# An attention and two-mixer kernel: first chunk's normalisation traced with heads 23 to 28, third batch's Fourier stage not hurried, last sums on VectorE

## The chip, the cores and the metric

One core of a Trainium2 chip. TensorE (PE) multiplies, VectorE (DVE), ScalarE (ACT) and GpSimd (POOL) work on tiles of 128 partitions, SyncE (SP) and others issue DMAs. The metric is the time of one execution on the device, in microseconds (us). The kernel before took 980.12 us (median of three runs, 977.31 to 981.54). About 0.5% (4.9 us) is what a measurement of this kernel can tell from no change.

## The reference

```python
x = attention(q, k, v, f)          # 4 batches, 8 heads, 576 positions, 64 wide; scores get a decay from cumsum(log f), causal softmax
# first mixer
X = np.fft.fft(np.fft.fft(x, axis=1), axis=2)
u = x + np.real(X)
un = (u - mean(u)) / np.sqrt(var(u) + 1e-06)         # over the 512 features
x = u + np.maximum(un @ w_ch1, 0.0) @ w_ch2          # 512 -> 2048 -> 512
# second mixer
theta = x @ w_theta
y = w_tok_r @ (x * cos(theta)) + w_tok_i @ (x * sin(theta))
u = x + y
out = u + np.maximum(u @ w_ch, 0.0)
```

## The kernel before

Features lie on partitions and positions along the free axis. The tile `u` (128 x 4 x 2304 floats) holds the result of the Fourier stage of all four batches, 576 columns each, from then on to the end.

The source is traced into one instruction list per engine. A planner orders each list: an instruction whose inputs and buffers are there may be placed ahead of others that were traced before it, those traced earlier (or marked `high_priority`) go first where both could start. On the chip each engine works through its own list in order and stops at an instruction that waits.

Phase 1 (`phase1`, lines 456 to 538) runs over n = -1 to 32. Turn n traces the scores of head n+1 (`score_units`: two matmul lines L232 and L233, the minimum on VectorE L241, Exp on ScalarE L246), the transposes of head n (`turn_units`, L271 and L274) and, every second turn, the product with v of a pair of heads (`av_units`, L303). After the pair, `evac_pair` scales it (L329, L335); for every odd pair it moves two rows by DMA through SP and forms the sum E and the difference O of the two pairs on GpSimd (L348, L350). After four pairs the Fourier stage of that batch (`fft_units`) starts as a generator. Each pass of the inner loop calls `pull()`, which takes one step of `rows` (evac_pair), one of `fft`, and on every third call one of `norm`. The Fourier stage folds E and O (L377, L381), splits them (L379 to L386), multiplies along the features (L406, L417) and along the positions (L429), and adds into `u` (L437 to L453), of which L447 is on GpSimd.

At n = 29 (line 510) the loop pulls until the Fourier stage of the third batch has been traced to its end. Only then its tiles E, O, yh, yl and zh can be taken for the normalisation of chunk 0. There are six chunks of 384 columns; chunk 0 lies in the first batch. `norm_units` (L689 to L716): three sums on GpSimd (L694 to L696), the mean by a matmul (L700), four subtractions on VectorE (L702), two squares on ScalarE (L705), three more sums on GpSimd (L706, L708), and the variance by three small matmuls (L713). `norm_end` follows: Sqrt on ScalarE (L720), reciprocal (L723), the spread of the three columns by matmuls (L725), and for each of four feature blocks a product (L732), a cast (L733) and a remainder (L734).

At n = 31 the pool of the heads' inputs closes and the weight loads open in its place: `decode` fetches half a weight block (L544, two `raw` buffers), takes it apart on ScalarE (L558), VectorE (L560, L561, L563, L565) and again ScalarE and VectorE (L570, L572). Phase 2 (`phase2`) traces the rest of the last batch's Fourier stage and then the matrix products of the first mixer, chunk by chunk, four weight blocks at a time: `ffn1` (L745, then the h tile by ACT L750 and DVE L751) and `ffn2` (L759, sums into u at L767). Phase 3 is the second mixer; the change does not touch it.

Of the kernel before, what the change touches and what calls it, by code (L numbers as in the profile page):

```python
# [8 lines left out]
F32 = mybir.dt.float32  # L9
# [3 lines left out]
AF = mybir.ActivationFunctionType  # L13
ALU = mybir.AluOpType
# [3 lines left out]
B, H, S, D = 4, 8, 576, 64  # L18
NP = 4
NF = 16  # L20
CH = 384
# [34 lines left out]
class Net:  # L56
    def __init__(self, ctx, tc, ins, out):
        self.ctx, self.tc, self.nc = ctx, tc, tc.nc
        self.i, self.out = ins, out
        nc = self.nc  # L60
        self.base = ctx.enter_context(tc.tile_pool(name="base", bufs=1))
        self.psa = ctx.enter_context(tc.tile_pool(name="psa", bufs=3, space=PSUM))
        self.psb = ctx.enter_context(tc.tile_pool(name="psb", bufs=3, space=PSUM))
        self.pt = ExitStack()
        self.pst = self.pt.enter_context(tc.tile_pool(name="pst", bufs=1, space=PSUM))
        self.nout = 0
        self.u = self.base.tile([128, 4, B * S], F32, name="u")
        self.ident = self.base.tile([128, 128], F32, name="ident")
        self.mean = self.base.tile([128, 128], F32, name="mean")
        nc.gpsimd.memset(self.mean, 1.0 / 512.0)  # L70
        self.eps = self.base.tile([128, 1], F32, name="eps")
        nc.gpsimd.memset(self.eps, 1e-6)
        self.un = {}
        self.stash = {}
        self.sdram = ctx.enter_context(tc.tile_pool(name="sdram", bufs=1, space=DRAM))
# [245 lines left out]
        yield  # L321
        done(m, T, R)

    def evac_pair(self, p, R, T):
        nc = self.nc
        k = p // 2
        if p % 2 == 0:
            self.X = R
            nc.vector.tensor_tensor(R, T[:, 256:832], R, ALU.mult)  # L329
            if k == 0:  # L330
                self.EO = [self.c1.tile([128, 2, S], F32, tag=x, name=x, bufs=2) for x in ("E", "O")]
            return
        X, (E, O) = self.X, self.EO
        Y = R
        nc.vector.tensor_tensor(Y, T[:, 256:832], R, ALU.mult)  # L335
        if k == 0:
            self.x384 = self.fdram.tile([1, S], F32, tag="x384", name="x384", bufs=2)
            nc.sync.dma_start(self.x384, Y[64:65])
            nc.sync.dma_start(Y[64:65], Y[0:1])
            nc.gpsimd.memset(Y[0:1], 0.0)  # L340
        else:
            self.x256 = self.c1.tile([1, S], F32, tag="x256", name="x256", bufs=1)
            nc.sync.dma_start(self.x256, Y[64:65])
            nc.sync.dma_start(Y[64:65], Y[0:1])
            nc.sync.dma_start(Y[0:1], self.x384)
        for _ in range(4):
            yield
        nc.gpsimd.tensor_tensor(E[:, k], X, Y, ALU.add)  # L348
        yield
        nc.gpsimd.tensor_tensor(O[:, k], X, Y, ALU.subtract)  # L350
        yield

    def fft_units(self, b, E, O, rows):
        nc = self.nc
# [36 lines left out]
        yh = w.tile([128, 3, 258], F32R, tag="yh", name="yh", bufs=1)  # L391
        yl = w.tile([128, 3, 258], F32R, tag="yl", name="yl", bufs=1)
# [4 lines left out]
        for s, (s0, me, mo) in enumerate(st):  # L397
            ps = self.bank_b()
# [33 lines left out]
        for t in range(2):  # L432
            ea = w.tile([128, S], F32, tag="ee", name="ea", bufs=1)
            oa = w.tile([128, S], F32, tag="oo", name="oa", bufs=1)
            ps = self.bank_b()
            fsum(ps, 128, yh, yl, cs, 128 * t, 128 * t + 128)
            nc.vector.scalar_tensor_tensor(ea[:, 0:289], E[:, t, 0:289], 0.5, ps[:, 0:289], ALU.mult, ALU.add)  # L437
            yield
            nc.vector.scalar_tensor_tensor(ea[:, 289:576], E[:, t, 289:576], 0.5, ps[:, 287:0:-1], ALU.mult, ALU.add)
            yield  # L440
            ps = self.bank_b()
            fsum(ps, 128, zh, zl, ss, 128 * t, 128 * t + 128)
            nc.vector.scalar_tensor_tensor(oa[:, 0:289], O[:, t, 0:289], -0.5, ps[:, 0:289], ALU.mult, ALU.add)
            yield
            nc.vector.scalar_tensor_tensor(oa[:, 289:576], O[:, t, 289:576], -0.5, ps[:, 287:0:-1], ALU.mult, ALU.subtract)
            (nc.vector if b == B - 1 or 1 >> t & 1 else nc.gpsimd).tensor_tensor(u[:, t, :], ea, oa, ALU.subtract)
            nc.gpsimd.tensor_tensor(u[:, 2 + t, :], ea, oa, ALU.add)  # L447
            for _ in range(1 if b == B - 1 or t else 7):
                yield
        ps = self.bank_b()  # L450
# [5 lines left out]
    def phase1(self):  # L456
        pair, heads = self.p1_open()
        NH = B * H
        pairs, heads, raws = {0: pair}, dict(enumerate(heads)), {}
        fft = None  # L460
        self.tick = 0
        rows, norm, av = iter(()), iter(()), iter(())

        def pull():
            nonlocal fft
            next(rows, 0)
            self.tick += 1
            if self.tick % 3 == 0:
                next(norm, 0)
            if (self.tick % 5 or n > 24) and fft is not None and next(fft, 0) == 0:  # L470
                fft = None

        def done(m, T, R):
            nonlocal rows, fft
            for _ in rows:
                pass
            rows = self.evac_pair(m % NP, R, T)
            next(rows, 0)
            if m % NP == NP - 1:
                fft = self.fft_units(m // NP, *self.EO, rows)  # L480

        for n in range(-1, NH + 1):
            a = self.score_units(heads[n + 1], (n + 1) % 2) if n + 1 < NH else iter(())
            prep = self.rest if n < 0 else iter(())
            if n + 2 < NH:
                p, g = divmod(n + 2, 2)
                if n == 0:
                    pairs[1] = self.load_pair(1)
                if n >= 0:
                    heads[n + 2] = dict(pair=pairs[p], g=n + 2)  # L490
                    prep = self.prep_units(n + 2, pairs[p], raws.pop(n + 2), heads[n + 2])
                if n > 0 and g == 1 and p + 1 < B * NP:
                    pairs[p + 1] = self.load_pair(p + 1)
            if n + 3 < NH:
                raws[n + 3] = self.load_head(n + 3)
            m, odd = divmod(n - 2, 2)
            if m >= 0 and not odd:
                T = self.bank_t()
                av = self.av_units(m, [heads[2 * m], heads[2 * m + 1]], T, pairs[m]["rz"], done)
            t = self.turn_units(heads[n]) if 0 <= n < NH else iter(())  # L500
            if n == NH - 1:
                self.p1a.close()
                self.p2_open()
                self.load(0)
                self.load(1)
            k = n - 2
            if 0 <= k < 4:
                for j in range(2):
                    self.load_dft(2 * k + j, f(heads[n]["hi"][0:1, 0, 0:2]))
            if n == NH - 3:  # L510
                while fft is not None:
                    pull()
                t1 = self.c1.tile([128, 2, CH], F32, tag="E", name="uc1", bufs=2)
                t2 = self.c1.tile([128, 2, CH], F32, tag="O", name="uc2", bufs=2)
                t3 = self.c1.tile([128, 2, CH], F32, tag="yh", name="s12", bufs=1)
                t4 = self.c1.tile([128, 2, CH], F32, tag="yl", name="sq", bufs=1)
                t5 = self.c1.tile([128, 4], F32, tag="zh", name="rs", bufs=1)
                norm = self.norm_units(0, ((t1, t2), t3[:, 0], t3[:, 1], t4, t5))
            live = True
            while live:  # L520
                live = False
                for g_ in (t, av, a):
                    if next(g_, 0) is None and (g_ is not av or n >= NH - 1):
                        live = True
                next(prep, 0)
                pull()
                if n >= NH - 1:
                    self.fill(2)
            for _ in prep:
                pass  # L530
        for _ in norm:
            pass
        self.p1b.close()
        for _ in rows:
            pass
        self.pt.close()
        self.pso = self.ctx.enter_context(self.tc.tile_pool(name="pso", bufs=2, space=PSUM))
        return fft
# [150 lines left out]
    def norm_units(self, c, temps):  # L689
# [22 lines left out]
        for k in range(3):  # L712
            nc.tensor.matmul(  # L713
                ps[:, 508 + k : 509 + k], s1[:, 128 * k : 128 * k + 128], self.mean[:, 0:1], start=True, stop=True
            )
        yield from self.norm_end(c, uc, rs, ps)  # L716

    def norm_end(self, c, uc, rs, ps):
        nc = self.nc
# [467 lines left out]
```

## Time and profile before

| what | value |
|---|---|
| median of three runs | 980.12 us (977.31 to 981.54) |
| the profiled execution | 974.18 us, its span 972.4 us |
| PE busy | 905.1 us (93% of the span) |
| DVE busy | 643.3 us (66%) |
| ACT busy | 426.1 us (44%) |
| POOL busy | 314.7 us (32%) |
| granted TensorE clock, mean of the span | 0.978 of full speed |

Shares of the whole span hide the stages. Phase 1 ends near 282 us, the first mixer has its first matmul at 284.05 us, and from about 369 us on PE is busy without a break to the end. Rows of the timeline give start and length in us, engine, line, operation, output and input; a bracket at the end is how long the engine stood idle before it, and what released it.

### The profile page before, as it was taken

Reading aid. Unit: us, or ns where it says so; the run is one execution under the profiler, and the core shown is the slowest. Engines: PE = TensorE matmul, PEld = TensorE weight load, DVE = VectorE, ACT = ScalarE, POOL = GpSimd, SP = SyncE. Lnnn points to the kernel's source line nnn. Section 1 sums busy time; section 2 is a strip of 40 time slices with the busy share of each in tenths; the row PEclk is TensorE's granted clock in tenths of the full one; section 3 lists DMA queues with packets and bytes.
Section 4 is the critical chain, followed back from the end, with each engine's and each line's share of the span. In section 5 each row is a group of like instructions: output and inputs, shape, how many; then the busy total and the mean of one; then the engine's idle time right before and its main releaser. Section 6 shows DMA issues by size and latency. Waiting matters only on the chain.

```text
span 972.4 us, 15900 instructions
## 1 busy us (share of the span) xinstructions
PE 905.1 (93%) x5960; PEld 850.8 (87%) x5960; DVE 643.3 (66%) x1503; ACT 426.1 (44%) x1038; POOL 314.7 (32%) x376
## 2 busy tenths in 40 slices
PE   3888898997978898999999999999999999999998
PEld 3667677776757798999999999999999999999998
DVE  7766777878789786535664466535677765746554
ACT  5777677767463342312322122212345534525331
POOL 4755457367433344200000000000014644525330
PEclk9998899999988999999999999999999999999999
DMA  4643223232132121002224022333420000010001
GB/s 145 200 131 123 70 86 102 89 101 67 36 108 67 44 87 44 1 1 77 76 65 145 30 87 87 112 108 106 138 62 1 1 25 26 2 37 14 25 26 49
DMA packets 24336, 68.04 MB, mean 70 GB/s; under 512 B 3534, under 2 KB 6990, under 8 KB 24260
## 3 DMA queue, kind: packets, MB, share of 16 engines
q1 hardware_dynamic: 20420, 62.52, 19.6%
q0 software_dynamic: 3120, 3.33, 1.4%
q10 hardware_dynamic: 720, 1.18, 0.4%
q8 instruction: 47, 0.77, 0.3%
q14 instruction: 29, 0.24, 0.1%
HBM read 57.92 MB, written 9.07 MB: 69 GB/s over the span
## 4 chain that ended last, share of the span: by engine, by line
PE 67%; DVE 18%; ACT 7%; issue 3%; POOL 2%; DMA 2%; ACTq 0%; DVEq 0%; POOLq 0%; SPq 0%
PE pa L745 19%; PE pb L759 11%; PE po L759 8%; PE pb L966 5%; PE pa L977 4%; PE pa L930 4%; PE pt L303 3%; ACT P L246 3%; PE po L966 3%; DVE P L241 2%; PE pb L271 2%; PE pa L232 2%; PE pa L233 2%; PE pb L429 1%; DVE kl L211 1%
## 5 line engine op out<-in xcount | busy, mean ns | idle before, releaser
L745 PE MATMUL pa<-un,wf 128*128 128x384 f32 x1152 | 222.8, 341 | 6.3 <-ACT wf L570 4.2
L745 PEld LDWEIGHTS pa<-un,wf 128*128 128x128 f32 x1152 | 204.4, 191 | 8.5 <-ACT wf L570 5.1
L751 DVE SCALAR_TENSOR_TENSOR h<-pa,h 128x384 fp32r<-128x384 f32 x96 | 53.1, 556 | 146.0 <-ACT h L750 146.0
L759 PE MATMUL pb<-h,wf 128*128 128x384 f32 x660 | 134.3, 336 | 0.3 <-DVE u L767 0.3
L759 PEld LDWEIGHTS pb<-h,wf 128*128 128x128 f32 x660 | 116.3, 188 | 0.9 <-DVE u L767 0.6
L750 ACT ACTIVATE h<-pa 128x384 fp32r<-128x384 f32 x96 | 46.8, 489 | 152.8 <-PE pa L745 152.7
L246 ACT ACTIVATE P<-P,mn 128x512 f32<-128x512 f32 (+4 forms) x160 | 95.7, 600 | 39.8 <-DVE mn L241 39.3
L759 PE MATMUL po<-h,wf 128*128 128x384 f32 x492 | 103.4, 339 | 4.1 <-DVE h L751 3.0
L232 PE MATMUL pa<-hi 128*128 128x448 f32 (+2 forms) x192 | 71.2, 390 | 30.8 <-DVE mn L241 16.1
L241 DVE CUSTOM_DVE_ANT_0 P<-pa,mask 128x512 f32<-128x512 f32 (+4 forms) x160 | 77.7, 510 | 30.6 <-PE pa L233 26.1
L966 PE MATMUL pb<-wtk,z 128*128 128x288 f32 x513 | 97.0, 294 | 0.0
L922 POOL COPY xd<-u 128x64 f32<-128x64 f32 x32 | 7.1, 265 | 272.2 <-DVE u L767 264.0
L759 PEld LDWEIGHTS po<-h,wf 128*128 128x128 f32 x492 | 87.5, 189 | 5.8 <-DVE h L751 3.4
L271 PE MATMUL pb<-ident,P 128*128 128x128 f32 x480 | 82.6, 288 | 7.4 <-ACT PT L274 4.3
L956 POOL TENSOR_TENSOR z<-kra,z 128x256 fp32r<-128x256 f32 x72 | 53.8, 767 | 86.8 <-ACT z L955 86.8
L966 PEld LDWEIGHTS pb<-wtk,z 128*128 128x128 f32 x513 | 79.2, 188 | 0.0
L966 PE MATMUL po<-wtk,z 128*128 128x288 f32 x351 | 75.1, 295 | 1.1 <-POOL z L956 1.1
L232 PEld LDWEIGHTS pa<-hi 128*128 128x128 f32 x192 | 38.7, 204 | 39.7 <-DVE mn L241 19.8
L271 PEld LDWEIGHTS pb<-ident,P 128*128 128x128 f32 x480 | 58.5, 147 | 14.0 <-ACT PT L274 6.4
L233 PE MATMUL pa<-kl,q 66*128 66x448 f32 (+2 forms) x192 | 63.4, 365 | 3.3 <-DVE kl L211 3.2
L930 PE MATMUL pa<-wf,xs 128*128 128x256 f32 x456 | 64.0, 289 | 0.0
L966 PEld LDWEIGHTS po<-wtk,z 128*128 128x128 f32 x351 | 57.4, 188 | 1.8 <-POOL z L956 1.6
(201 smaller groups left out, 1689.5 us busy)
## 6 DMA issues: line engine op xcount, KB each, us to landing
raw<-in_qk SPq DMA_DIRECT2D x31, 576.0 KB, 3.8
raw<-in_wf SPq DMA_DIRECT2D x32, 512.0 KB, 4.2
raw<-in_wtk SPq DMA_DIRECT2D x18, 288.0 KB, 2.8
v<-in_vp SPq DMA_DIRECT2D x16, 320.0 KB, 3.6
out<-ob SPq DMA_DIRECT2D x12, 288.0 KB, 2.1
dft<-in_dft POOLq DMA_DIRECT2D x8, 346.0 KB, 4.7
raw<-in_wth SPq DMA_DIRECT2D x4, 512.0 KB, 4.0
st_wth<-raw SPq DMA_DIRECT2D x4, 512.0 KB
```

The lines of the kernel that those rows point to most:

```text
L232: nc.tensor.matmul(t[:, 0 : b - a], hi[:, 1, q], hi[:, 0, a:b], start=True, stop=False)
L233: nc.tensor.matmul(t[:, 0 : b - a], q2[:, q], kl[:, g, a:b], start=False, stop=True)
L241: nc.vector.tensor_tensor_reduce(out=p[:, a:b], in0=t[:, 0 : b - a], in1=self.mask[:, S - n0 - 128 + a : S - n0 - 128 + b], scale=1.0, sca ...
L246: nc.scalar.activation(p, p, AF.Exp, bias=lowest, scale=-1.0, accum_out=zs[:, g, i : i + 1])
L271: nc.tensor.transpose(ps[:, o : o + 128], src, self.ident)
L745: nc.tensor.matmul(ps[:, 0:CH], t[:, l, 128 * d : 128 * d + 128], un[r][:, d], start=n == 0, stop=n == 11)
L750: nc.scalar.activation(h[:, 0], ps[:, 0:CH], AF.Relu)
L751: nc.vector.scalar_tensor_tensor(h[:, 1], ps[:, 0:CH], 0.0, f(h[:, 0]), ALU.max, ALU.subtract)
L759: nc.tensor.matmul(outs[d], t[:, l, 128 * d : 128 * d + 128], h[:, r], start=k % G == 0 and n == 0, stop=k % G == G - 1 and n == 2,)
L930: nc.tensor.matmul(th, xs[:, l, d], self.wth[d][:, r, 256 * hf : 256 * hf + 256], start=n == 0, stop=n == 11)
L956: nc.gpsimd.tensor_tensor(z[:, 1], t, f(z[:, 0]), ALU.subtract)
L966: nc.tensor.matmul(acc[k][th], z[:, l, 128 * k : 128 * k + 128], self.wtk[kt][:, r, 288 * th : 288 * th + 288], start=first and i == 0 and ...
```

## The change

`evac_pair` gets a flag for the very last pair; with it, E and O are formed on VectorE. The last batch's L447 goes to VectorE too. The block at n = 29 goes: the third batch's Fourier stage is pulled at its ordinary pace, and whatever is left of it at n = 32 is pulled then. The first part of chunk 0's normalisation is traced from n = 23 on (`norm_early`), one step in three pulls; its temporary tiles are columns of `u` that belong to the third and fourth batches. From n = 31 the rest is traced (`norm_late`), one step in each pull. The small tile `rs0` holds its scale.

```diff
+        self.rs0 = self.base.tile([128, 4], F32, name="rs0")
...
-    def evac_pair(self, p, R, T):
+    def evac_pair(self, p, R, T, last):
...
-        nc.gpsimd.tensor_tensor(E[:, k], X, Y, ALU.add)
-        yield
-        nc.gpsimd.tensor_tensor(O[:, k], X, Y, ALU.subtract)
+        sums = nc.vector if last else nc.gpsimd
+        sums.tensor_tensor(E[:, k], X, Y, ALU.add)
+        yield
+        sums.tensor_tensor(O[:, k], X, Y, ALU.subtract)
...
-            nc.gpsimd.tensor_tensor(u[:, 2 + t, :], ea, oa, ALU.add)
+            (nc.vector if b == B - 1 else nc.gpsimd).tensor_tensor(u[:, 2 + t, :], ea, oa, ALU.add)
...
-            if self.tick % 3 == 0:
+            if self.tick % 3 == 0 or n >= NH - 1:
                 next(norm, 0)
...
-            rows = self.evac_pair(m % NP, R, T)
+            rows = self.evac_pair(m % NP, R, T, m == B * NP - 1)
...
-            if n == NH - 3:
-                while fft is not None:
-                    pull()
-                t1 = self.c1.tile([128, 2, CH], F32, tag="E", name="uc1", bufs=2)
-                t2 = self.c1.tile([128, 2, CH], F32, tag="O", name="uc2", bufs=2)
-                t3 = self.c1.tile([128, 2, CH], F32, tag="yh", name="s12", bufs=1)
-                t4 = self.c1.tile([128, 2, CH], F32, tag="yl", name="sq", bufs=1)
-                t5 = self.c1.tile([128, 4], F32, tag="zh", name="rs", bufs=1)
-                norm = self.norm_units(0, ((t1, t2), t3[:, 0], t3[:, 1], t4, t5))
+            if n == NH - 9:
+                norm = self.norm_early()
+            if n == NH - 1:
+                for _ in norm:
+                    pass
+                norm = self.norm_late()
+            while n == NH and fft is not None:
+                pull()
...
+    def norm_early(self):
+        nc = self.nc
+        u = self.u[:, :, 0:CH]
+        free2, free3 = (self.u[:, :, b * S : (b + 1) * S] for b in (2, 3))
+        uc2 = [free3[:, 2 * k : 2 * k + 2, 0:CH] for k in range(2)]
+        uc = [free3[:, d, 0:CH] for d in range(4)]
+        sq, s2 = free2[:, 0:2, 0:CH], free2[:, 2, 0:CH]
+        s1 = free3[:, 0:3, CH : CH + 128]
+        cut = lambda x: x.rearrange("p (k c) -> p k c", c=128)
+        self.early = (uc, s1)
+        nc.gpsimd.tensor_tensor(s1, cut(u[:, 0]), cut(u[:, 1]), ALU.add)
+        yield
+        nc.gpsimd.tensor_tensor(s2, u[:, 2], u[:, 3], ALU.add)
+        yield
+        nc.gpsimd.tensor_tensor(s1, s1, cut(s2), ALU.add)
+        yield
+        ps = self.bank_b()
+        nc.tensor.matmul(ps[:, 0:CH], self.mean, s1, start=True, stop=True)
+        for d in range(4):
+            nc.vector.tensor_tensor(uc[d], u[:, d], ps[:, 0:CH], ALU.subtract)
+        yield
+        for k in range(2):
+            nc.scalar.activation(sq, uc2[k], AF.Square)
+            yield
+            if k:
+                nc.gpsimd.tensor_tensor(s2, sq[:, 0], sq[:, 1], ALU.add)
+            else:
+                nc.gpsimd.tensor_tensor(s1, cut(sq[:, 0]), cut(sq[:, 1]), ALU.add)
+            yield
+        nc.gpsimd.tensor_tensor(s1, s1, cut(s2), ALU.add)
+        yield
+
+    def norm_late(self):
+        uc, s1 = self.early
+        ps = self.bank_b()
+        for k in range(3):
+            self.nc.tensor.matmul(
+                ps[:, 508 + k : 509 + k], s1[:, k], self.mean[:, 0:1], start=True, stop=True
+            )
+        yield from self.norm_end(0, uc, self.rs0, ps)
```

## Rows read from the trace of the kernel before

**Rows 1.** Stages: window, its length, busy us by engine, TensorE clock, DMA share, GB/s
```profile
200.00:252.00 52.00, 45.41 (x329) 36.20 (x328) 40.13 (x114) 37.06 (x107) 30.74 (x36) 0.97 0.24 78
252.00:269.00 17.00, 15.73 (x104) 12.87 (x104) 13.66 (x45) 8.36 (x27) 13.13 (x15) 1.00 0.00 0
269.00:300.00 31.00, 21.68 (x132) 17.43 (x129) 26.69 (x49) 18.78 (x41) 10.54 (x12) 0.81 0.31 103
300.00:369.00 69.00, 61.45 (x366) 57.99 (x365) 58.69 (x109) 25.27 (x48) 25.29 (x19) 0.96 0.19 62
369.00:972.00 603.00, 595.53 (x3902) 592.82 (x3900) 355.38 (x766) 195.29 (x428) 125.02 (x158) 1.00 0.17 54
```
**Rows 2.** PE's waits, 252 to 369 us: who for whom, total us, times, longest
```profile
PE pa L745 <- ACT wf L570: 4.2, 2, 2.2
PE po L759 <- DVE h L751: 3.0, 1, 3.0
PE pa L745 <- ACT un L733: 1.6, 1, 1.6
...
PE pa L283 <- POOL wide L252: 1.0, 1, 1.0
```
**Rows 3.** Timeline of VectorE, 274 to 300 us
```profile
274.90 0.69 DVE L274 COPY PT<-pb 128x512 f32<-128x512 f32 x1 [3.15 <-PE pb L271]
...
282.91 1.48 DVE L732 TENSOR_TENSOR uc<-uc,pb 128x384 f32<-128x384 f32 x3
...
292.13 0.55 DVE L734 TENSOR_TENSOR un<-uc,un 128x384 fp32r<-128x384 f32 x1
293.15 3.23 DVE L560 TENSOR_SCALAR a<-a 128x512 f32<-128x512 f32 x1 [0.47 <-ACT a L558]
```
**Rows 4.** Timeline of GpSimd, 285 to 318 us
```profile
292.31 1.03 POOL L373 TENSOR_TENSOR xl<-xx,xh 1x290 fp32r<-1x290 f32 x1 [5.58 <-ACT xh L372]
293.31 1.41 POOL L348 TENSOR_TENSOR E<-X,Y 128x576 f32<-128x576 f32 x1
...
309.65 1.85 POOL L447 TENSOR_TENSOR u<-ea,oa 128x576 f32<-128x576 f32 x1 [13.55 <-DVE oa L445]
313.99 3.13 POOL L447 TENSOR_TENSOR u<-ea,oa 128x576 f32<-128x576 f32 x1 [2.49 <-DVE oa L445]
```
**Rows 5.** Timeline of VectorE, 300 to 318 us
```profile
303.98 0.42 DVE L560 TENSOR_SCALAR a<-a 128x512 f32<-128x512 f32 x1
...
310.14 1.98 DVE L446 TENSOR_TENSOR u<-ea,oa 128x576 f32<-128x576 f32 x1
...
314.20 0.74 DVE L446 TENSOR_TENSOR u<-ea,oa 128x576 f32<-128x576 f32 x1
...
316.03 1.36 DVE L560 TENSOR_SCALAR a<-a 128x512 f32<-128x512 f32 x1
```
**Rows 6.** Timeline of PE: twice the same matmuls, 289 and 355 us
```profile
289.26 5.81 PE L745 MATMUL pa<-un,wf 128*128 128x384 f32 x17 [2.08 <-ACT wf L570]
...
355.02 2.24 PE L745 MATMUL pa<-un,wf 128*128 128x384 f32 x12
```
**Rows 7.** Timeline of ScalarE, 261 to 280 us
```profile
261.63 0.59 ACT L287 COPY Y<-pb 128x512 f32<-128x512 f32 x1 [7.15 <-PE pb L283]
...
270.39 0.40 ACT L246 ACTIVATE P<-P,mn 128x128 f32<-128x128 f32 x1
...
278.81 1.28 ACT L720 ACT_TABLE_LOAD   x1
```
**Rows 8.** One line each: count, ns min/median/max, first and last start, forms
```profile
L694 POOL TENSOR_TENSOR s<-u x5: 997/1008/1664, 259.5 to 385.3; 128x384 f32<-128x384 f32 x5
...
L700 PE MATMUL pb<-s,mean x10: 483/484/553, 266.6 to 389.9; 128*128 128x384 f32 x10
...
L702 DVE TENSOR_TENSOR uc<-u,pb x20: 540/547/555, 269.5 to 392.8; 128x384 f32<-128x384 f32 x20
...
L705 ACT ACTIVATE sq<-uc x10: 835/846/851, 270.8 to 394.4; 128x768 f32<-128x768 f32 x10
```

## The prediction

> **What bounds the kernel now.** I read the table of stages first, for one question: where is PE not the limit? From 369 us on PE is busy 595.5 of 603 us at full clock; there nothing can be won but by taking work from PE, and the change takes none [rows 1]. Up to 252 us the heads run with PE at 45.4 of 52 us, VectorE at 40.1 and ScalarE at 37.1, so no engine is full and each head hangs on a chain through three of them. Between lie the two stretches that the change is about. From 269 to 300 us PE is idle for 31 - 21.7 = 9.3 us and has a mean clock of 0.81; from 300 to 369 us it is idle for 69 - 61.5 = 7.5 us. In the same two stretches VectorE is busy 26.7 of 31 and 58.7 of 69 us, 85 to 86%: there it is the fullest engine beside PE, and its queue decides when weights, h tiles and normalised chunks are ready.
>
> The second view is PE's waits there [rows 2]. The longest are for a decoded weight (4.2 us), for an h tile (3.0 us) and for the normalised chunk (1.6 us). The third is VectorE's timeline behind these waits [rows 3]. Its last product and remainder for chunk 0 (L732, L734) are spread from 282.91 to 292.68 us among the decode steps, so the chunk is complete only then, and the decode steps lie behind it in turn. Then a decode step, L560, runs 3.23 us where the same shape takes 0.42 us elsewhere [rows 3, 5]. It is this step that the h tile's L751 waits behind.
>
> **The change part by part.** I make the sum against the profiled execution, 974.18 us (span 972.4 us and 1.8 us around it). That is 6 us under the median of 980.12 us and under the lowest of the three runs, so I carry over the difference and not the time.
>
> *The end of chunk 0's normalisation leaves the crowded stretch.* On VectorE `norm_end` is four products and four remainders of one shape; the row has three products in 1.48 us, 0.49 each, and a remainder at 0.55 us, so 4 x 0.49 + 4 x 0.55 = 4.2 us, all of it between 282.91 and 292.68 us before [rows 3]. In the new kernel its inputs are there when n = 31 is traced, so it can fill VectorE's idle 3.15 us just ahead of 274.90 us and gaps among the last heads. Bounds: nothing, if the planner leaves it behind the decode steps, to 4.2 us, and 1.6 us more for PE's wait for the chunk if the weights are there [rows 2, 3]. I take 4.0, near the upper end, because the idle place of 3.15 us is a row of just this engine and time. The first part (L702) also leaves: 4 x 0.547 = 2.2 us [rows 8], but it lay in front of that idle place, so I count nothing for it here.
>
> *The last sums change engines.* On GpSimd E takes 1.41 us, and O, its twin, ends at 296.1 us; it is in that time that L560 is stretched by 3.23 - 0.42 = 2.8 us, and it ends 0.3 us behind them [rows 3 to 5]. The two L447 on GpSimd, of 1.85 and 3.13 us, lie over L446 at 1.98 instead of 0.74 us (1.24 us lost) and over L560 at 1.36 instead of 0.42 us (0.94 us lost) [rows 4, 5]. So VectorE gets back 2.8 + 1.2 + 0.9 = 4.9 us and pays four ops of the shape of L446, 4 x 0.74 = 3.0 us: net 1.9 us. On the chain it is more: E and O take 1.5 us in place of 2.8 and don't stand behind L373, which kept GpSimd idle for 5.58 us and then ran 1.03 us [rows 4]. Added is a wait: E on VectorE waits for a row that SP's DMA brings, and behind it in VectorE's list stand decode steps; GpSimd was late itself, so the trace doesn't show that wait. Its bounds are 0 and the 3.0 us of PE's wait for h [rows 2], if all of the stretched step's place becomes waiting. I take the gain as 2.8 us, the stretch that stood in front of h; bounds 0 to 4.9.
>
> The Trainium skill, GPSIMD Engine Reference, Key points, says that GpSimd shares its SBUF interfaces with VectorE and contends with ops that have two SBUF inputs or run in a two-port mode. The trace agrees where L560 ends with O (3.23 against 0.42 us). It also speaks against the next part, which adds six sums on GpSimd; if each held VectorE for its whole length, the sum below would be 5 us less.
>
> *The early part moves into heads 23 to 28.* There it issues six sums on GpSimd, 6 x 1.01 = 6.1 us, two passes of L700 on PE, 2 x 0.48 = 1.0 us, four L702 on VectorE, 2.2 us, and two squares on ScalarE, 2 x 0.85 = 1.7 us; no DMA [rows 8]. Before, the same work ran from 259 to 276 us beside the last heads, so it is moved, not added; what can be lost is where it lands. GpSimd is busy 30.7 of 52 us in the heads, VectorE 40.1 [rows 1]. On GpSimd it is moved past the heads' preparation (hi, q), and a sum that waits for a square would hold that. Bounds: -1 us (it fits the gaps, and PE's wait of 1.0 us for `wide` behind these sums goes [rows 2]) to 6.1 us (every sum holds VectorE). I take a cost of 1.0 us, near the cheap end, because all engines have gaps there and the steps are traced one in three pulls.
>
> *The third batch isn't hurried.* Before, the matmuls of its last steps run as a block, and ScalarE stands idle for 7.15 us ahead of 261.63 us [rows 7]. But PE is busy 15.7 of 17 us in that stretch [rows 1], so spreading the block wins at most the 1.3 us that PE was idle, and behind it the waits of the two last heads, 1.0 us for `wide` and some of the 9.3 us after 269 us. I take 2.0 us; bounds 0 and 3.3 (the 1.3 and two waits of a microsecond). What is late next is the first weight: its buffers open with the last score, so any gain here moves it too.
>
> The sum: 4.0 + 2.8 + 2.0 - 1.0 = 7.8, say 8 us. From 980.1 us that is 972.1 us; I predict 972. With PE full behind 369 us, a lead is kept to the end. The forecast's own range is a gain of 4 to 12 us, 968 to 976.
>
> **The rivals.** *The weights set the start anyway (977).* PE's longest wait is for a weight, 4.2 us, not for the chunk, 1.6 us [rows 2]. Then the 4.0 us of the first part buy nothing, some of the last sums goes into the wait for the DMA, and the gain is about 3 us. For it: the waits' order. Against it: the decode steps share VectorE with the chunk.
>
> *The heads pay (986, slower).* If the chain of each head, minimum to Exp to transposes, is what ends last in heads 23 to 28, the added 2.2 us on VectorE and 1.7 on ScalarE and 6.1 us of held VectorE lie on it: 10.0 us. With a gain that shrinks to 4 us, since the last heads and weights start later, the kernel is 6 us slower. It decides from the point where the heads lose more than the 8.8 us that the other parts gain. For it: no engine is full there, and the chain is long [rows 1]. Against it: gaps of 7 to 21 us on each engine in 52 us.
>
> *Sqrt comes too early (975).* The table of Sqrt is loaded once, 1.28 us, behind the last Exp [rows 7]. In the new kernel Sqrt's input is ready some heads sooner, and the planner may place it ahead of the last Exps; then Exp's table and later Sqrt's have to be loaded again, two loads, 2.6 us: a gain of 5.4 us. The Trainium skill, ScalarE: Activation LUTs, Table sets, asks to finish all of one table set before switching; no run here shows a switch back.
>
> *The clock too (967).* From 289 to 295 us 17 matmuls take 5.81 us, 0.342 each, where 12 take 2.24 us, 0.187 each, at full clock [rows 6]; the granted clock of the stretch is 0.81, so part of it ran at the lower level of 1.2 GHz, and PE stood idle for 2.08 us just before. If the gaps close so far that it keeps 2.4 GHz, 17 x 0.155 = 2.6 us and as much around it come on top: a gain of 13 us.
>
> *That the change doesn't do what it says* (the planner leaves the early part where it was) gives the gain of the first rival.
>
> **How the numbers follow.** Forecast 0.40, weights or nothing moved 0.16, heads pay 0.18, Sqrt too early 0.14, clock too 0.12. Faster by over 0.5% means under 975.2 us: 0.36 of the forecast, the clock's 0.12 and 0.08 of Sqrt, together 0.56. Within 0.5%: 0.04 + 0.06 + 0.16 + 0.02 of the heads' case, 0.28. Slower: 0.16. The range takes the clock's case and the bounds of the forecast with 4 us below 967, and reaches up to 982, the milder half of the heads' case: 963 to 982.
>
> **What would show it.** In the new trace chunk 0's L734 should end before 283 us and before the second weight pair; E and O should take 0.75 us on VectorE and no L560 there more than 1 us; L447 should be gone from GpSimd behind 300 us; the last Exp should be no later than 270.8 us [rows 7], and PE's idle time from 269 to 369 us should fall from 16.9 to some 10 us. I am wrong if the last Exp is later by several us, if a second load of the Exp table shows, if VectorE stands idle in front of E, or if PE's wait for a weight grows by what the other waits lose.

## The result, and the profile after

The changed kernel takes 987.43 us (median of six runs, 983.44 to 989.55); beside it the kernel before took 977.40 us (six runs, 976.07 to 981.54). The ratio is 1.0091, with a 95% interval of 1.0065 to 1.0116: slower by 0.9%. I had forecast 972 us and a range of 963 to 982. The profiled execution took 987.49 us, its span is 985.7 us.

One caution for all that follows: the profiled executions of the kernel before (974.18 us, and 974.12 us when it was profiled again as e5) lie 3.2 and 5.6 us under the medians that were measured beside them (977.40 and 979.72 us), while those of the other kernels lie between 3.2 us under and 3.0 us over theirs. So a difference against the trace of before comes out some 4 us too large. I use traces for places and ratios for prices.

The stages after, to be held against [rows 1] (window, length, busy us of PE, PEld, DVE, ACT, POOL, granted clock, DMA share, GB/s):

```profile
200.00:252.00 52.00, 43.57 (x305) 35.00 (x303) 41.55 (x110) 36.54 (x101) 34.14 (x40) 0.93 0.25 79
252.00:269.00 17.00, 16.83 (x121) 13.90 (x118) 11.61 (x30) 7.84 (x23) 4.48 (x5) 0.93 0.15 50
269.00:300.00 31.00, 26.89 (x184) 20.60 (x184) 25.27 (x64) 19.01 (x47) 9.80 (x13) 0.94 0.27 85
300.00:369.00 69.00, 59.74 (x328) 55.19 (x328) 57.66 (x112) 27.43 (x52) 16.69 (x16) 0.90 0.21 69
```

From 269 to 300 us PE is busier than before (26.9 against 21.7 us), yet it is not further: it is doing heads there that were finished before. From 300 to 369 us it idles 9.3 us where it idled 7.5; in both stretches together that is 13.4 us, not the 10 that I had forecast. PE's waits from 252 to 369 us (who for whom, total, times, longest), beside [rows 2]:

```profile
PE pb L408 <- ACT eh L381: 3.3, 1, 3.3
PE pa L787 <- ACT wf L571: 2.4, 1, 2.4
...
PE pa L787 <- ACT un L775: 1.1, 1, 1.1
```

The wait for an h tile, the 3.0 us that I meant to take away, is gone; a wait of 3.3 us for `eh`, the first fold of the last batch's Fourier stage, has come in its place. The landmarks of the traces tell when the time is lost (starts in us; for the v product its end):

| landmark | before | after | e11 | e9 | e6 | e8 |
|---|---|---|---|---|---|---|
| Exp of head 19 | 159.96 | 163.42 | 159.12 | 158.70 | 160.53 | 157.88 |
| Exp of head 22 | 185.99 | 192.08 | 187.20 | 186.27 | 188.57 | 188.09 |
| Exp of head 28 | 233.71 | 240.39 | 236.60 | 234.69 | 237.08 | 236.75 |
| Exp of head 30 | 263.82 | 270.23 | 265.21 | 269.01 | 269.96 | 269.51 |
| last Exp | 270.39 | 279.79 | 271.78 | 275.58 | 276.53 | 276.09 |
| first weight DMA | 269.02 | 279.83 | 270.42 | 274.23 | 274.64 | 274.19 |
| last v product ends | 281.59 | 293.89 | 282.70 | 286.49 | 287.52 | 287.07 |
| first Fourier matmul of the last batch | 300.21 | 315.40 | 299.81 | 302.72 | 309.69 | 302.45 |
| span | 972.4 | 985.7 | 971.6 | 974.5 | 980.1 | 975.6 |

(e6, e8, e9 and e11 are experiments below.) The first 6 us are lost before head 22, at 185 us, although the change is traced from n = 23 on. There the trace shows what stands in GpSimd's list. First GpSimd (start, length, line, a bracket for idle time and its releaser), then VectorE and PE, of the changed kernel; the line between them has the shortest, middle and longest of the two L212 in ns, and their starts:

```profile
156.20 1.00 POOL L729 TENSOR_TENSOR u<-u 128x384 f32<-128x384 f32 x1
157.17 0.98 POOL L731 TENSOR_TENSOR u<-u 128x384 f32<-128x384 f32 x1
158.13 0.72 POOL L253 TENSOR_SCALAR wide<-rz 128x640 f32<-128x640 f32 x1
158.82 0.98 POOL L733 TENSOR_TENSOR u<-u 128x384 f32<-128x384 f32 x1
159.78 0.66 POOL L205 TENSOR_SCALAR hi<-raw 128x576 fp32r<-128x576 f32 x1
...
156.94 5.24 DVE L212 SCALAR_TENSOR_TENSOR kl<-raw,hi 64x576 fp32r<-64x576 f32 x2
L212 DVE SCALAR_TENSOR_TENSOR kl<-raw,hi x2: 1208/2655/4102, 156.9 to 161.0; 64x576 fp32r<-64x576 f32 x2
...
161.19 0.79 PE L234 MATMUL pa<-kl,q 66*128 66x448 f32 x3 [3.85 <-DVE kl L212]
...
162.12 4.61 PE L304 MATMUL pt<-PT,v 128*64 128x256 f32 x28
```

L729, L731 and L733 are the three early sums. The last additions into the first batch's columns end at 152.8 us; the planner placed the sums soon behind them, where their inputs are there, long before n = 23. They stand ahead of L205, which prepares the next head, and VectorE's pair of remainders L212 beside them takes 5.24 us: the first 4.10, the second 1.21 us. PE waits 3.85 us, and its matmul L234 starts 0.15 us behind the end of the first of the pair (161.04 us). L205 is late too, but it had ended at 160.44 us, so it is not what ended this wait. Behind that idle time the clock granted to PE falls:

```profile
155.00:162.00 7.00, 2.78 (x19) 2.31 (x19) 7.00 (x11) 4.37 (x14) 6.92 (x12) 1.00 0.00 0
162.00:166.00 4.00, 4.00 (x22) 2.20 (x22) 1.68 (x8) 1.90 (x5) 2.86 (x3) 0.57 0.83 258
```

0.57 from 162 to 166 us is mostly the lower level of 1.2 GHz, and the 28 matmuls of L304 take 4.61 us there (2.92 in e3, below).

The second loss is at the end of the heads. PE, VectorE, ScalarE and SP's queue of the changed kernel:

```profile
274.12 2.93 PE L304 MATMUL pt<-PT,v 128*64 128x256 f32 x28
...
277.51 0.43 PE L431 MATMUL pb<-dft,yh 128*128 128x290 f32 x2
...
277.71 0.42 DVE L242 CUSTOM_DVE_ANT_0 P<-pa,mask 128x256 f32<-128x256 f32 x1 [3.25 <-PE pa L234]
...
279.79 0.40 ACT L247 ACTIVATE P<-P,mn 128x128 f32<-128x128 f32 x1
...
279.83 17.43 SPq L545 DMA_DIRECT2D raw<-in_wf  x5
...
279.90 0.53 PE L431 MATMUL pb<-dft,zh 128*128 128x290 f32 x2 [0.19 <-ACT PT L275]
...
289.97 3.92 PE L304 MATMUL pt<-PT,v 128*64 128x256 f32 x28
```

A product with v and the Fourier matmuls that are no longer hurried now stand among the last scores; VectorE idles 3.25 us for a score, the last Exp starts at 279.79 us (before at 270.39 [rows 7]), and 0.04 us later the first weight is fetched. But 6.7 of these 9.4 us are there at head 28 already, and from head 28 to the last Exp the hurried kernel e6 needs as long as the changed one (39.4 us; before 36.7). What the unhurried stage itself costs shows behind the last Exp: PE still has its matmuls L431 to do until 282.58 us, ahead of the last head's transposes, and the last product with v ends 14.1 us behind the last Exp, in e6 11.0 us. The third is VectorE behind that, the counterpart of [rows 3]:

```profile
288.80 0.55 DVE L774 TENSOR_TENSOR u<-u,pb 128x384 f32<-128x384 f32 x1
...
297.12 0.56 DVE L776 TENSOR_TENSOR un<-u,un 128x384 fp32r<-128x384 f32 x1
...
298.52 0.75 DVE L336 TENSOR_TENSOR Y<-pt,Y 128x576 f32<-128x576 f32 x1
...
310.20 0.56 DVE L793 SCALAR_TENSOR_TENSOR h<-pa,h 128x384 fp32r<-128x384 f32 x1 [1.58 <-ACT h L792]
310.70 0.69 DVE L573 TENSOR_TENSOR wf<-a,wf 128x512 fp32r<-128x512 f32 x1
311.31 0.75 DVE L350 TENSOR_TENSOR E<-X,Y 128x576 f32<-128x576 f32 x1
```

Chunk 0's end still runs from 288.80 to 297.68 us among the decode steps, no narrower than before (282.91 to 292.68 us). The last product Y, ready with the v product at 293.89 us, stands behind it and starts 4.6 us later; E, which needs Y's rows by DMA, starts at 311.31 us.

### The profile page after: what moved, and what is told of

The parts are those of the page before. It is cut to its first block, busy times and chain, and to the rows that moved or that the text cites. A ratio compares the mean times of both kernels' runs of the same rounds, so it can differ in the third digit from the quotient of the medians.

```text
span 985.7 us, 15898 instructions
## 1 busy us (share of the span) xinstructions
PE 916.4 (93%) x5960; PEld 858.0 (87%) x5960; DVE 648.8 (66%) x1507; ACT 426.6 (43%) x1038; POOL 305.2 (31%) x372
## 4 chain that ended last, share of the span: by engine, by line
PE 70%; DVE 16%; ACT 7%; issue 3%; POOL 2%; DMA 1%; SPq 0%; ACTq 0%; DVEq 0%; POOLq 0%
PE pa L787 19%; PE pb L801 11%; PE po L801 8%; PE pb L1008 5%; PE pa L1019 4%; PE pa L972 4%; PE pt L304 4%; PE po L1008 3%; ACT P L247 3%; PE pb L272 2%; PE pb L431 2%; PE pa L233 2%; DVE P L242 2%; DVE kl L212 2%; PE pa L234 1%
## 5 line engine op out<-in xcount | busy, mean ns | idle before, releaser
L801 PE MATMUL pb<-h,wf 128*128 128x384 f32 x660 | 136.8, 340 | 0.2 <-DVE u L809 0.2
L801 PEld LDWEIGHTS pb<-h,wf 128*128 128x128 f32 x660 | 118.6, 190 | 0.8 <-DVE u L809 0.6
L247 ACT ACTIVATE P<-P,mn 128x256 f32<-128x256 f32 (+4 forms) x160 | 95.7, 601 | 40.9 <-DVE mn L242 40.3
L234 PE MATMUL pa<-kl,q 66*128 66x448 f32 (+2 forms) x192 | 64.0, 365 | 5.6 <-DVE kl L212 5.5
```

The source lines that it names most:

```text
L234: nc.tensor.matmul(t[:, 0 : b - a], q2[:, q], kl[:, g, a:b], start=False, stop=True)
L247: nc.scalar.activation(p, p, AF.Exp, bias=lowest, scale=-1.0, accum_out=zs[:, g, i : i + 1])
L801: nc.tensor.matmul(outs[d], t[:, l, 128 * d : 128 * d + 128], h[:, r], start=k % G == 0 and n == 0, stop=k % G == G - 1 and n == 2,)
```

## The experiments

The names are those of the table. "Ratio" is always to the kernel before, with its 95% interval.

**e1 and e11: the last sums alone.** Before, with only this:

```diff
+        sums = nc.vector if last else nc.gpsimd
+        sums.tensor_tensor(E[:, k], X, Y, ALU.add)
...
+            (nc.vector if b == B - 1 else nc.gpsimd).tensor_tensor(u[:, 2 + t, :], ea, oa, ALU.add)
```

> Edit: the kernel before, with the last E, O and both last L447 on VectorE and nothing else changed. The prediction's term for these sums was a gain of 2.8 us: 0.997 of the kernel before, L560 at 293 us back from 3.23 to about 0.42 us, Fourier matmuls of the last batch 2 to 3 us sooner than 300.2 us. Rival (VectorE's list is full there and E comes behind decode steps): E starts no sooner than 293 us and the time is the same or up to 2 us longer, 1.000 to 1.002.

> The kernel of e1 again, beside e9 and e10 on the same chip, so that these are read against it. Theory: 0.992 again, 0.990 to 0.995. If the gain of e1 was partly chance, 0.996 to 0.998 (the two profiled executions of e1 and of the kernel before have the same span).

Measured: 972.79 us, ratio 0.9923 (0.9900 to 0.9947), and again 972.24 us, 0.9940 (0.9918 to 0.9962). This part works, and by more than the 2.8 us of the sum (5.9 and 7.5 us by the ratios; the traces give less, the end of the last v product to the first Fourier matmul is 16.7 and 17.1 us, before 18.6). VectorE of e1:

```profile
294.90 0.76 DVE L561 TENSOR_SCALAR a<-a 128x512 f32<-128x512 f32 x1 [0.18 <-ACT a L559]
295.58 0.75 DVE L349 TENSOR_TENSOR E<-X,Y 128x576 f32<-128x576 f32 x1
296.25 0.74 DVE L351 TENSOR_TENSOR O<-X,Y 128x576 f32<-128x576 f32 x1
```

The decode step that took 3.23 us beside GpSimd's E and O [rows 3] takes 0.76. e1 beats both kernels.

**e4: the changed kernel with the sums back on GpSimd.** The two lines above undone in the changed kernel.

> Edit: the changed kernel, with the last E, O and both L447 back on GpSimd; early normalisation and the unhurried stage stay. By the prediction's term the sums on VectorE gain 2.8 us, so this is slower than the changed kernel: 1.012 of the kernel before. Rival (on VectorE E and O stand behind decode steps, 2.8 us after their data came): this is faster than the changed kernel by 2 us, 1.007.

Measured: 985.78 us, 1.0065 (1.0041 to 1.0088). Inside this change the same edit gains nothing and looks like a loss (1.0091 against 1.0065; the intervals overlap). GpSimd of e4:

```profile
307.64 1.42 POOL L350 TENSOR_TENSOR E<-X,Y 128x576 f32<-128x576 f32 x1 [4.31 <-DMA Y<-x]
```

On GpSimd E starts as its row lands, 14.8 us behind the end of the last v product (292.84 us in e4). On VectorE it stands behind h and a decode step and starts 17.4 us behind it (311.31 and 293.89 us, above).

**e3: the first two early sums held back.** An order without a semaphore, behind the head preparation that is traced just before them on the same engine:

```diff
+            self.behind = nc.gpsimd.tensor_scalar(q2[0:64], ...)
...
+        self.hold(nc.gpsimd.tensor_tensor(s1, cut(u[:, 0]), cut(u[:, 1]), ALU.add))
+        self.hold(nc.gpsimd.tensor_tensor(s2, u[:, 2], u[:, 3], ALU.add))
```

> Edit: the changed kernel, with the first two sums of the early normalisation held in GpSimd's list behind the q copy traced just ahead of them at n = 23; nothing else. Theory (the planner placed the three sums in front of hi of head 20, which costs 2.9 us there and the rest of 5.5 us through a lower TensorE clock): the Exps of head 22 start where they did before, within 1 us (the changed kernel has them 6.1 us late), and the time is 5 us shorter than the changed kernel's: 1.004 of the kernel before. Rival (the sums cost as much wherever they stand in the heads): head 22 is on time but head 28 is late by 6 us all the same, 1.009.

Measured: 982.22 us, 1.0029 (1.0012 to 1.0047). The same place in e3, GpSimd, VectorE and PE:

```profile
155.44 0.72 POOL L253 TENSOR_SCALAR wide<-rz 128x640 f32<-128x640 f32 x1
156.14 0.66 POOL L205 TENSOR_SCALAR hi<-raw 128x576 fp32r<-128x576 f32 x1
...
156.17 2.37 DVE L212 SCALAR_TENSOR_TENSOR kl<-raw,hi 64x576 fp32r<-64x576 f32 x2
L212 DVE SCALAR_TENSOR_TENSOR kl<-raw,hi x2: 1207/1219/1231, 156.2 to 157.3; 64x576 fp32r<-64x576 f32 x2
...
157.55 0.79 PE L234 MATMUL pa<-kl,q 66*128 66x448 f32 x3 [0.99 <-DVE kl L212]
...
158.49 2.92 PE L304 MATMUL pt<-PT,v 128*64 128x256 f32 x28
...
208.46 1.00 POOL L736 TENSOR_TENSOR u<-u 128x384 f32<-128x384 f32 x1
```

The first sum now runs at 208.46 us (L736 is its line here), 52 us later than in the changed kernel. With the sums gone from 156 us the pair takes 2.37 instead of 5.24 us, PE waits 0.99 instead of 3.85 us, L304 takes 2.92 instead of 4.61 us, and the granted clock from 162 to 166 us is 1.00. The early placing cost 0.62% (1.0091 less 1.0029); beside a hurried third batch the same edit is worth 0.41% (e2 and e6 below).

**e2: the third batch hurried again.**

```diff
+            if n == NH - 3:
+                while fft is not None:
+                    pull()
```

> Edit: the changed kernel, with the third batch's Fourier stage pulled to its end at n = 29 as before; early normalisation and sums on VectorE stay. Theory (the unhurried stage put its matmuls and a product with v ahead of the last scores): the last Exp comes 3 to 4 us sooner than the 279.8 us of the changed kernel, the first weight load follows it, and the time is 4 us shorter than the changed kernel's: 1.005 of the kernel before. Rival (all the loss lies in heads 19 to 22 and behind the last head): no difference to the changed kernel, 1.009.

Measured: 983.59 us, 1.0054 (1.0035 to 1.0073). The unhurried stage, which I had put down as a gain of 2.0 us, costs 0.37% here (the intervals of 1.0091 and 1.0054 overlap). With the sums held the same edit is worth 0.16%, less than the uncertainty (1.0029 for e3, 1.0013 for e6 below). The theory's place was wrong: the last Exp comes 1.7 us sooner, at 278.13 us, not 3 to 4; from there to the end of the last product with v it is 11.0 us in e2 and e6, and 14.1 us in the changed kernel and in e3. A microsecond of these 3.1 us is that product itself: it takes 3.92 us in the changed kernel (above), at a granted clock of 0.75 from 290 to 294 us, and 2.93 us in e2, at 1.00 from 286 to 290 us.

**e5: the kernel before again**, for the caution above.

> Edit: none, the kernel before with a profile of its own. Its first profiled execution was some 4 us under the median of its runs. Expected: a span near 977 us, and the first weight load between 269 and 273 us; where the other microseconds lie (heads, clock, or behind the first matmul of the mixer) tells how far stretches of single traces may be compared.

Measured: 974.12 us in the profiled execution, span 972.3 us, not the 977 expected: the low trace came again.

**e6: held and hurried.** Both edits.

> Edit: the changed kernel with both mendings at once: the early sums held behind n = 23 in GpSimd's list, and the third batch pulled to its end at n = 29. What is left of the change is the early normalisation at its place and the sums on VectorE. If the two losses add up: 1.009 - 0.004 - 0.006 = 0.999 of the kernel before, that is 7 us slower than with the sums alone (0.992), because chunk 0's products stand in VectorE's list ahead of the last Y product. If the early normalisation in itself gains the 4 us of the prediction: 0.988.

Measured: 980.22 us, 1.0013 (0.9996 to 1.0031), near the additive 0.999. What is left of the change in e6 is the early normalisation and the sums; it should be as good as e1 or better, and is 0.7 to 0.9% behind.

**e7 and e8: the last Y product sooner.** The changed kernel (e7) and e6 (e8) with:

```diff
+        with self.tc.high_priority(400 if last else 0):
+            nc.vector.tensor_tensor(Y, T[:, 256:832], R, ALU.mult)
```

> Edit: the changed kernel, with the last Y product (L336) traced at high priority; in VectorE's list it comes 11 places earlier, behind the last v product by 1 to 2 us in place of 4.6 us. Theory (the late Y product holds the row DMAs and so the last Fourier stage): Fourier matmuls start 3 us sooner and the time is 3 us shorter than the changed kernel's, 1.006. Rival (that stretch is bound by the decode steps anyway): 1.009.

> Edit: as the run with both mendings, and the last Y product at high priority too. Theory: 3 us shorter than without the priority, 0.996 of the kernel before, still slower than the sums alone (0.992). Rival (decode steps bind): as without, 0.999.

Measured: e7 986.88 us, 1.0081 (1.0059 to 1.0104); e8 979.03 us, 0.9994 (0.9977 to 1.0012). In e8 SP's queue reads

```profile
287.96 0.50 SPq L345 DMA_DIRECT2D x<-Y  x1
289.64 0.50 SPq L346 DMA_DIRECT2D Y<-Y  x1
```

right behind the v product (287.07 us), where the changed kernel's first row move went at 299.31 us, 5.4 us behind its v product. The last batch's Fourier matmuls start 7.2 us sooner than in e6, the span is 4.5 us shorter, but by the ratios only 0.19% is gained in e8 and 0.10% in e7, less than the intervals. The place of Y is a real wait with a small price.

**e9: a copy of the early part beside e1.** `norm_early` is traced and held as in e3, drained ahead of the hurry, and used by nobody:

```diff
+            if n == NH - 9:
+                norm = self.norm_early()
...
             if n == NH - 3:
+                for _ in norm:
+                    pass
+                norm = iter(())
                 while fft is not None:
```

> The kernel of e1 (before, with the last sums on VectorE) with a copy of the early part beside it: norm_early is traced from n = 23, its first two sums held behind the head preparation traced just before, and its results are used by nobody; chunk 0 is still normalised at the old place. So this prices the early part in the heads by itself, with the order at the end as in e1. Theory: its sums stand in GpSimd's list ahead of E and O of the third batch's last pair, which start some 2.5 us later (233.6 us in e1, 236.0 us in e8), and the Fourier stage that is hurried at n = 29 waits for them: last heads 3 to 3.5 us later than in e1, ratio to before 0.996 (e1: 0.9923). Rival: the early part fits into the gaps, and what separates e6 and e8 from e1 is made at the end: 0.992 to 0.993. Second rival: the early part is the whole of the difference between e6 and e1: 1.001.

Measured: 976.39 us, 0.9969 (0.9951 to 0.9987), beside 0.9940 for e11 on the same chip: 0.29%, as the theory had it, each of the two uncertain by 0.2%. GpSimd and PE, first e11, then e9:

```profile
228.12 0.78 POOL L371 TENSOR_TENSOR xx<-x 1x287 f32<-1x287 f32 x1
...
232.66 1.41 POOL L349 TENSOR_TENSOR E<-X,Y 128x576 f32<-128x576 f32 x1
...
240.72 0.74 PE L407 MATMUL pb<-dft,eh 128*128 128x258 f32 x2
```

```profile
228.16 1.40 POOL L756 TENSOR_TENSOR u<-u 128x384 f32<-128x384 f32 x1
...
230.28 1.00 POOL L760 TENSOR_TENSOR u<-u 128x384 f32<-128x384 f32 x1
...
233.97 1.42 POOL L349 TENSOR_TENSOR E<-X,Y 128x576 f32<-128x576 f32 x1
...
243.15 0.80 PE L407 MATMUL pb<-dft,eh 128*128 128x258 f32 x2 [3.45 <-ACT PT L274]
```

At 228 us the two kernels stand level on GpSimd. Two early sums (L756, L760) go ahead of the third batch's last E, which starts 1.3 us later (the theory had 2.5); its Fourier stage starts 2.4 us later, and head 30, which stands behind the hurried stage, 3.8 us later (table). The last 1.5 us come with the clock: behind PE's 3.45 us of idle time the product with v of 28 matmuls takes 4.40 us, in e11 2.93. So the early part does cost in the heads. That the late E alone makes the 2.4 us is argued, not shown: the fold `eh` is only 0.65 us later (240.27 against 239.62 us), and the bracket of the Fourier matmul names a copy of head 28's transposes.

**e10: the early part behind that O.** In e8, `norm_early` is traced at n = 28, its sums held behind O of the third batch's last pair, where GpSimd idles beside the hurried stage:

```diff
-            if n == NH - 9:
+            if n == NH - 4:
                 norm = self.norm_early()
...
+        self.behind = sums.tensor_tensor(O[:, k], X, Y, ALU.subtract)
```

> e8 (sums on VectorE, third batch hurried, last Y product with priority) with the early part in another place: its sums are held behind O of the third batch's last pair and traced at n = 28, so that they run beside the hurried Fourier stage, where GpSimd stood idle for 4.6 and 7.9 us in e8. Theory (what the early part costs is the delay of E and O): the head 30 starts its Exps some 3 us earlier against head 28 than in e8 (28.5 us behind it as in e1, not 32.8), ratio 0.996 or less (e8: 0.9994), down to 0.991 if the shorter end of e8 (15.4 us from the last product with v to the first Fourier matmul, 16.7 in e1) is kept on top. Rival: six sums cost the same wherever they stand in the heads: 0.999 again.

Measured: 987.40 us, 1.0093 (1.0067 to 1.0118). Both expectations fell. ScalarE of e10:

```profile
265.74 0.84 ACT L752 ACTIVATE u<-u 128x768 f32<-128x768 f32 x1 [3.28 <-DVE u L749]
...
275.77 0.59 ACT L288 COPY Y<-pb 128x512 f32<-128x512 f32 x1 [6.41 <-PE pb L284]
```

Here E itself starts at 240.33 us, behind `wide` in the list, so it was not freed at all; and the squares and second sums come at 265 to 271 us, ahead of the third batch's additions into `u`, which must wait since the squares lie in its columns. Head 31 starts its Exps 11.9 us behind head 30 (3.4 in e8). The kernel shows a third bad place, but it doesn't tell whether the delay of E alone is the price; for that e9 is the nearest evidence.

**e12: chunk 0's end left out.** What is left out says the text:

> The kernel of e1 and e11 (before, with the last sums on VectorE) with the end of chunk 0's normalisation left out: the four products are gone, the casts read the centred values straight away and the remainders are replaced by zeros that GpSimd sets. The sums, the mean, the squares and the Sqrt stay. VectorE loses 4.2 us in the crowded stretch and the chunk is complete some heads sooner, so this is the most that an early normalisation could give there at no cost elsewhere. Theory of the prediction (this end is worth 4.0 us): e11's 0.994 less 0.4%, 0.990. Rival (the weights set the start): PE's first mixer matmul starts no more than 2 us sooner and the wait for the weight grows; 0.992 to 0.994.

Measured: 973.45 us, 0.9966 (0.9945 to 0.9987); span 968.5 us, against 971.6 and 972.3 of e11 and e1. PE in e1, then in e12, with two of e12's windows:

```profile
286.11 0.44 PE L746 MATMUL pa<-un,wf 128*128 128x384 f32 x1 [1.79 <-ACT un L734]
286.97 1.67 PE L746 MATMUL pa<-un,wf 128*128 128x384 f32 x6 [0.41 <-DVE un L735]
291.30 5.28 PE L746 MATMUL pa<-un,wf 128*128 128x384 f32 x17 [2.67 <-ACT wf L571]
```

```profile
282.70 2.34 PE L750 MATMUL pa<-un,wf 128*128 128x384 f32 x12
...
288.53 4.59 PE L750 MATMUL pa<-un,wf 128*128 128x384 f32 x12 [1.22 <-ACT wf L571]
...
282.00:288.00 6.00, 4.60 (x28) 3.66 (x24) 3.88 (x8) 1.85 (x4) 1.10 (x2) 1.00 0.31 124
288.00:294.00 6.00, 4.88 (x13) 3.86 (x14) 5.18 (x10) 2.61 (x5) 1.25 (x1) 0.52 0.54 175
```

The wait for the chunk goes, the mixer starts 2.7 us sooner than in e11 (the last Exp had come 1.9 us sooner), and then PE waits for the next weight all the same, and its next 12 matmuls take 4.59 instead of 2.34 us at a granted clock of 0.52. From the end of the last v product to the first Fourier matmul it is 15.3 us against 17.1 in e11: 1.8 us. But that product took 4.62 us in e12, at a granted clock of 0.57 from 278 to 282 us, and 2.92 in e11; from the last Exp it is 27.5 against 28.0 us, 0.5 us. The times show no gain at all (0.9966 against 0.9923 and 0.9940). So this term is worth 0.5 to 1.8 us by the trace and nothing that the times show, not 4.0; the theory of the prediction fell, and the rival with the weights is nearer, though the wait for the weight became shorter (1.22 against 2.67 us), not longer.

## Why the prediction was wrong

Five kernels lead from the part that works to the whole change; the differences of their ratios are the prices, each uncertain by some 0.3%, so that each is clear of nothing by little or not at all, while their sum of 1.5% is plain. The step to e6 is more than one edit, since it also drops the old first part, which e9 still does:

| step | ratio | price |
|---|---|---|
| sums alone (e11) | 0.9940 | |
| the early part in the heads, held (e9) | 0.9969 | +0.29% |
| its results used, end traced from n = 31 (e6) | 1.0013 | +0.44% |
| sums no longer held (e2) | 1.0054 | +0.41% |
| third batch not hurried (the change) | 1.0091 | +0.37% |

Taken in the other order, by way of e3 (1.0029), the last two steps are 0.16% for the unhurried batch and 0.62% for the sums that aren't held.

*The early part, put down at a cost of 1.0 us, within -1 and 6.1.* This is the step that failed most: 0.29 + 0.41 = 0.70%, some 7 us (by the other order 0.29 + 0.62). I argued that "all engines have gaps there and the steps are traced one in three pulls". Gaps counted over 52 us don't say whether a sum stands ahead of a link of the chain, and where a step is traced doesn't say where it runs: three sums ran at 156 us. The mechanism is that of the rival *the heads pay*, whose 986 us is also next to the result, and what held head 19's scores was a VectorE operation held by GpSimd, as that rival has it. But its place was wrong by half (heads 19 to 22, not 23 to 28 alone), and its sum has a gain of 4 us from the other parts, which didn't come; that its 986 us is so near is luck. For the 0.29% of e9 the place is shown and the mechanism only argued. The Trainium skill's Key points in the GPSIMD Engine Reference, weighed in the prediction, agree with the row: a remainder of L212 that takes 1.2 us in e3 takes 4.10 us beside five GpSimd operations. I read the rule, priced it with "5 us less", and then took the cheap end.

*The third batch, put down as a gain of 2.0 us.* It costs 0.37%, 3.6 us, beside the sums that run early, and 0.16%, within the noise, beside held ones; a gain shows in neither. The bound "0 and 3.3" excluded a loss for no reason. PE did use the 1.3 us that it had idled (16.83 of 17 us), as I said; but the work it did there was not the work that ends last. The last head's transposes and the last product with v moved behind it (14.1 instead of 11.0 us from the last Exp), and the weights: their first DMA starts 3.6 us later than in e2, 0.9 us later in e3 than in e6. The prediction even named that the weights open with the last score, and drew only the good sign from it.

*The end of chunk 0's normalisation, put down as 4.0 us.* e12 puts it at 0.5 to 1.8 us in the trace. PE's longest wait was for a weight, not for the chunk [rows 2], as the rival *the weights set the start* has it. And the planner did not put the end into VectorE's idle time at 275 us: it stayed among the decode steps, and took the place of Y. That explains part of the 0.44% of e6; the priority in e8 gives 0.19% of it back. At the first Fourier matmul of the last batch e8 is level with e9 (302.45 and 302.72 us), and by its ratio it is still 0.25% behind. This rest I can't place with these runs, and its cause stays open.

*The last sums, put down as 2.8 us.* Right in sign and mechanism by themselves (e1, e11: 5.9 to 7.5 us), and mis-sized. In the change they gave nothing that the times show (e4): the wait that I named, E for its row on VectorE with decode steps about it, turned up the other way round, as E waiting behind h and `wf`. The signs named for this part did come: E and O take 0.75 us on VectorE, and no decode step there is stretched to 3 us.

*Sqrt too early* didn't come: the table is loaded once, at 284.62 us, behind the last Exp. *The clock too* went against the change: 0.57 at 162 us, 0.90 from 300 to 369 us, where it was 0.96 [rows 1]. Of the signs that I named, "the last Exp is later by several us" was the one that came (9.4 us).

## What to carry to other kernels

An instruction that is moved to an earlier place in the source may run earlier still: ask from when on its inputs are there, and what stands behind it in that engine's list at that time, above all on an engine that "has gaps" but prepares the next step of a chain. More work for a busy engine in a stretch is only a gain if it is the work that ends last there; a bound of a gain that has no room for a loss needs a reason. A chain of kernels that adds one edit at a time prices a mixed change where single traces, which scatter by some us, don't; but the price of an edit depends on what else is in the kernel (0.16 or 0.37% for the unhurried batch), so take the chain in a second order where you can.

## What the runs showed of the hardware

One pair of VectorE operations took 5.24 us beside five GpSimd operations that followed each other without a gap, and 2.37 us in the same place without the sums; the three sums on GpSimd kept their length (0.98 to 1.00 us). The stretch is not the sum of overlaps: the first of the pair took 4.10 us, to 0.6 us behind the end of the five, where L212 takes 0.75 us in the middle of its 32 runs. The loss isn't VectorE's alone: the sixth GpSimd operation, the q copy L211 beside the end of the pair, took 1.16 instead of 0.66 us, and in [rows 4] an L447 took 3.13 us where most take 1.43.

An idle time of 3.85 us on PE was followed by a granted clock of 0.57 for some 4 us, in which 28 matmuls took 4.61 instead of 2.92 us: the delay cost another 1.7 us on top. In e12 a chunk that came sooner was followed by 12 matmuls in 4.59 us at 0.52, where 12 had taken 2.34 us at 1.00; in e11, with the chunk late, the clock is 0.50 from 290 to 294 us too. Gaps and lead are not traded one for one.

Traces of one kernel repeat well (972.4 and 972.3 us for before, 972.3 and 971.6 for e1), but both profiled executions of before lie under its medians, by 3.2 and 5.6 us, while those of the other kernels scatter to both sides; why, these runs don't show.
